# Hashed attention with an expert layer on one core: the first head loaded and projected in two parts, and eight bit moves spread over twice the steps

## The chip, the cores and the metric

One NeuronCore of a Trainium2 chip. The metric is the device time of one execution in microseconds. A profile's *span*, from the first to the last instruction, is about 2 us shorter. Engines: PE is TensorE, DVE is VectorE, ACT is ScalarE, POOL is GpSimd, and SP only issues DMAs.

## The reference, cut to what matters

```
q_bits = (einsum('bhsd,dk->bhsk', q, proj) > 0)          # 6 sign bits per token
k_bits = (einsum('bhsd,dk->bhsk', k, proj) > 0)
mask   = q_bucket[:, :, :, None] == k_bucket[:, :, None, :]
attn   = softmax(where(mask, q @ k^T / 8, -1e9)); x = attn @ v    # B=4, H=8, S=768, D=64
g = h * sigmoid(h), h = x @ w_in; out = g @ w_out        # 3072 x 512 -> 2048 -> 512
```

## The kernel before: the parts that the change touches

The kernel appends the sign bits as extra rows to q and k, so that one matmul gives score and mask together. A *step* `w` is one score part of 512 columns (9 steps a head, 288 in all). Each step issues planned side work, then attention times v, then the score of three steps ahead. `vv` is v in f16 and `vs` the sum of v's blocks; for the first eight heads and the last one, one matmul of the constant `dmat` with `vs` goes ahead of attention times v. Before any of that, the first head must be loaded, transposed, projected, and its bits moved to their rows:

```
for i in range(2):                       # SP's queue
    load_first(i)                        # q and k of head i, whole
    load_v(0, slice(i, i + 1))
...
t_first(0, 0, nc.scalar.copy)            # 3 transposes + copy
t_first(0, 1, nc.vector.tensor_copy)
warm_up(2)
bt = proj_first(0)                       # 4 f32 projections + signs on DVE
v_unit(0, (0,))                          # POOL: vv and vs of v
... cast_first on ACT; bits_first on DVE, DVE, ACT, POOL
t_first(1, 0, nc.scalar.copy)            # head 1's transposes, before the first score on PE
t_first(1, 1, nc.vector.tensor_copy)
warm_up(3)
```

The other place is in the steady state. An h_ps buffer (three exist, shared with the projections) is free again only when DVE has made `g` from it:

```
plan(wp + (i if Q < 4 else 0),           # Q = 3: pairs 6 and 7, wp = 93
     lambda Q=Q, i=i: bits_unit((2 * Q, 2 * Q + 1), i // 2, i % 2))   # two DVE moves each
...
after.append(lambda: nc.vector.scalar_tensor_tensor(out=g..., in0=th, scalar=1.0, in1=hp, ...))
```

## Time and profile before

| | before |
|---|---|
| time, median of the first 3 runs (lowest to highest) | 304.26 us (304.14 to 304.9) |
| span of the profiled run | 302.6 us |
| PE busy | 297.0 us, 98% |
| first score | 8.31 us |
| h_ps held up by g | 0.84 us at 73.5 us |
| PE clock at full rate from (the trace's clock record) | 6.0 us |

The prediction below shows the lines and reads them. Warm-ups are matmuls that compute nothing.

### The profile page before, as it was taken

The numbers are of one execution on the slowest core, as the hardware profiler recorded it, in microseconds if no ns is written. First come the engines' busy times: TensorE is split into PE (matmuls) and PEld (weight loads), VectorE is DVE, ScalarE is ACT, GpSimd is POOL, SyncE is SP. The second block draws the span as 40 slices with busy tenths as digits, with TensorE's granted clock in tenths as the row PEclk, the third lists the DMA queues.
The fourth block names the chain that finished last, engine by engine and source line by source line (L and its number), as shares of the span: only waits on it lengthen the run. The fifth ranks groups of instructions, "written<-read, shape, count | busy, mean of one in ns | idle before, by whom it ended". The sixth has DMA issues, their size and how long they took to land.

```text
span 302.6 us, 7181 instructions
## 1 busy us (share of the span) xinstructions
PE 297.0 (98%) x2710; PEld 175.1 (58%) x2710; DVE 180.0 (59%) x344; ACT 210.1 (69%) x392; POOL 128.2 (42%) x203
## 2 busy tenths in 40 slices
PE   8999999998999999999999999999999999999996
PEld 3676755545665665555565665555566654446653
DVE  5797938899568454854695434954443442764332
ACT  5987989988887686878886766878877732452300
POOL 6589999386618561845149411765111100000000
PEclk9999999999999999999999999999999999999999
DMA  7999998999979828744068146011022003001112
GB/s 202 245 248 215 156 145 122 217 180 166 145 161 153 131 74 229 124 97 134 3 126 139 51 63 203 2 40 32 2 61 63 4 34 95 35 2 69 37 66 73
DMA packets 103170, 32.87 MB, mean 109 GB/s; under 512 B 90656, under 2 KB 100192, under 8 KB 103136
## 3 DMA queue, kind: packets, MB, share of 16 engines
q1 hardware_dynamic: 98752, 28.22, 43.3%
q0 software_dynamic: 4224, 4.19, 9.0%
q8 instruction: 21, 0.34, 0.5%
q14 instruction: 13, 0.11, 0.1%
q10 hardware_dynamic: 160, 0.00, 0.0%
HBM read 27.27 MB, written 6.29 MB: 111 GB/s over the span
## 4 chain that ended last, share of the span: by engine, by line
PE 89%; DVE 5%; DMA 2%; issue 1%; SPq 1%; ACT 1%; POOL 0%; DVEq 0%; ACTq 0%; POOLq 0%
PE o_ps L496 26%; PE h_ps L461 24%; PE s_ps L366 18%; PE o_ps L398 11%; PE bp_ps L281 3%; DMA v_sb<-in_v_dram 2%; PE tp_ps L185 2%; DVE g L470 2%; PE o_ps L482 1%; PE warm_ps L125 1%; SPq L92 1%; DVE qka L343 1%; PE bp_ps L225 1%; DVE qk L246 1%; PE tp_ps L198 0%
## 5 line engine op out<-in xcount | busy, mean ns | idle before, releaser
L369 ACT ACTIVATE u<-s_ps 128x512 f16<-128x512 f32 x288 | 157.0, 606 | 38.7 <-PE s_ps L366 38.3
L470 DVE SCALAR_TENSOR_TENSOR g<-th,h_ps 128x512 f16<-128x512 f32 x96 | 65.5, 686 | 74.8 <-ACT th L468 74.7
L461 PE MATMUL h_ps<-xT,win 128*128 128x512 f16 (+1 forms) x512 | 98.4, 325 | 0.8 <-DVE g L470 0.8
L398 PEld LDWEIGHTS <-u 128*128 128x128 f16 x1152 | 68.1, 98 | 42.2 <-ACT u L369 8.4
L496 PE MATMUL o_ps<-wout,g 128*128 128x512 f16 x368 | 91.6, 379 | 0.0
L468 ACT ACTIVATE th<-h_ps 128x512 f32<-128x512 f32 x96 | 57.9, 603 | 36.6 <-PE h_ps L461 33.9
L398 PE MATMUL o_ps<-vv,u 128*128 128x65 f16 x1152 | 82.6, 194 | 0.6 <-ACT u L369 0.4
L461 PEld LDWEIGHTS <-win 128*128 128x128 f16 x512 | 49.8, 98 | 31.4 <-issue 1.0
L418 POOL TENSOR_TENSOR x_pr<-osum,rec 128x384 f16<-128x384 f32 x23 | 19.0, 826 | 89.3 <-DVE rec L417 88.9
L496 PEld LDWEIGHTS <-g 128*128 128x128 f16 x368 | 35.8, 98 | 33.6
L366 PE MATMUL s_ps<-qka 71*128 71x512 f16 x192 | 52.7, 327 | 0.2 <-DVE qka L238 0.2
L366 PE MATMUL s_ps<-qkb 128*128 128x512 f16 x192 | 52.6, 326 | 0.0
L251 POOL TENSOR_SCALAR qka<-qk 64x1536 f16<-64x1536 f32 x15 | 22.0, 1466 | 11.4 <-DVE qk L246 5.6
L501 DVE TENSOR_SCALAR osb<-o_ps 128x512 f32<-128x512 f32 x23 | 15.9, 691 | 15.0 <-PE o_ps L496 15.0
L251 POOL TENSOR_SCALAR qkb<-qk 64x1536 f16<-64x1536 f32 x15 | 22.1, 1471 | 1.2
L262 POOL TENSOR_TENSOR vsa<-v_sb 128x192 f32<-128x192 f32 x32 | 19.0, 592 | 0.0
L260 POOL CAST vv<-v_sb 128x384 f16<-128x384 f32 x32 | 16.2, 507 | 0.9 <-DMA v_sb<-in_v_dram 0.5
L246 DVE STREAM_TRANSPOSE qk<-k_blk 128x768 f32<-128x768 f32 x10 | 15.8, 1582 | 0.3 <-issue 0.3
L246 DVE STREAM_TRANSPOSE qk<-q_blk 128x768 f32<-128x768 f32 x10 | 15.9, 1591 | 0.0
L366 PEld LDWEIGHTS <-qka 71*128 71x128 f16 x192 | 15.5, 97 | 0.8 <-ACT qka L238 0.7
L366 PEld LDWEIGHTS <-qkb 128*128 128x128 f16 x192 | 15.4, 97 | 0.0
L412 DVE TENSOR_TENSOR osum<-o_ps,vsum 128x390 f32<-128x390 f32 x23 | 13.0, 565 | 2.3
(70 smaller groups left out, 163.0 us busy)
## 6 DMA issues: line engine op xcount, KB each, us to landing
out_dram<-osb SPq DMA_DIRECT2D x23, 256.0 KB
v_sb<-in_v_dram SPq DMA_DIRECT2D x15, 384.0 KB
q_blk<-in_q_dram SPq DMA_DIRECT2D x40, 96.0 KB
k_blk<-in_k_dram SPq DMA_DIRECT2D x40, 96.0 KB
win<-in_moe_w_in_dram POOLq DMA_DIRECT2D x4, 512.0 KB, 6.6
wout<-in_moe_w_out_dram POOLq DMA_DIRECT2D x4, 512.0 KB, 6.9
q_sb<-in_q_dram SPq DMA_DIRECT2D x5, 384.0 KB
k_sb<-in_k_dram SPq DMA_DIRECT2D x5, 384.0 KB
```

What stands on the lines that cost most here:

```text
L246: nc.vector.transpose(out=dst, in_=qk_sb[p, "qk"[n]])
L251: nc.gpsimd.tensor_scalar(out=dst[rows, :], in0=qk32[p][rows, :], scalar1=CS, scalar2=1.0, op0=ALU.mult, op1=ALU.mult)
L260: nc.gpsimd.tensor_copy(out=vv[:, :, 0:D], in_=src)
L262: nc.gpsimd.tensor_tensor(out=sa, in0=src[:, 0:3], in1=src[:, 3:6], op=ALU.add)
L366: nc.tensor.matmul(sp[:, o0 : o0 + n], t[rows, S + jt * P : S + (jt + 1) * P], t[rows, c0 : c0 + n], start=True, stop=True)
L369: nc.scalar.activation(out=u, in_=sp, func=AF.Exp, scale=ESC)
L398: nc.tensor.matmul(o_ps[h][:, c0 // P + i, :], u[:, o0 + i * P : o0 + (i + 1) * P], vv[:, jt, :], start=(not direct(h) and w % NU == 0 and ...
L418: (nc.vector if direct(h) else nc.gpsimd).tensor_tensor(out=x_pr[p][:, :, par * D : (par + 1) * D], in0=o[:, 0:NJ, 0:D], in1=rec[:, :, Non ...
L461: nc.tensor.matmul(hp[:, j, :], w_in16[:, dt, ft * P : (ft + 1) * P], xT[4 * b + dt][:, c0 : c0 + n], start=(dt == 0), stop=(dt == NDT - 1))
L468: nc.scalar.activation(out=th, in_=hp, func=AF.Tanh, scale=0.5)
L470: after.append(lambda: nc.vector.scalar_tensor_tensor(out=g[ci][:, grp * f : (grp + 1) * f, :], in0=th, scalar=1.0, in1=hp, op0=ALU.add, o ...
L496: nc.tensor.matmul(o2[tt], g[ci][:, ft, ct * P : (ct + 1) * P], w_out16[:, ft, :], start=(ft == 0), stop=(ft == NFT - 1))
```

## The change

Its intent is to start the first score earlier by bringing two thirds of the first head first, and to keep DVE from delaying `g` in steps 93 to 96. The diff, cut to its core (cuts marked with `...`; among what is cut, the warm-ups come in smaller pieces and DVE zeroes one buffer behind the first head instead of ahead of it):

```
-    for i in range(2):
-        load_first(i)
-        load_v(0, slice(i, i + 1))
+    load_first(0, (slice(0, 4 * D),))              # SP: blocks 0 and 1 of q and k
+    load_v(0, slice(0, 1))
+    load_first(1)
+    load_v(0, slice(1, 2))
...
+    load_first(0, (slice(4 * D, NJ * D),))         # POOL: block 2, after ident
...
+    t_first(0, 0, act, xa);  casts of q (ACT);  warm_up(1)        # xa: blocks 0 and 1
+    t_first(0, 1, vec, xa);  casts of k (DVE);  warm_up(2)
+    bpa = proj_first(0, xa)
+    t_rest()                                       # 2 transposes, one copy on ACT
+    for e in range(2):
+        cast_first(0, 0, e, nc.scalar, xb)         # xb: block 2
+        cast_first(0, 1, e, nc.gpsimd, xb)
+    v_unit(0, (0,), "v")                           # POOL: vv alone
+    signs_first(0, bpa, xa)
+    bpb = proj_first(0, xb)
+    ... bit moves of xa (DVE, POOL, ACT), signs of xb, ACT's second move of xa, bit moves of xb
+    v_unit(0, (0,), "s")
+    t_first(1, 0, act); t_first(1, 1, vec); warm_up(1)
...
-        if j == 1:                                 # order of a head's score parts
+        if j == 2:
...
+        if direct(h) and w % NU == (0 if h else 4):   # head 0: dmat at step 4, not 0
...
-            plan(wp + (i if Q < 4 else 0),
+            plan(wp + {2: i, 3: 2 * i}.get(Q, 0),
```

More of the change, by code (lines that the diff above doesn't have):

```diff
@@ L72, in load_qk, with load_first @@
             qk_sb[p, n] = t
-    def load_first(h):
-        for n, src in (("q", q), ("k", k)):
-            if h == 0:
-                qk_sb[0, n] = ld.tile([P, 2, NJ * D], F32, tag=f"ld{n}", name=f"{n}_row")
-            nc.sync.dma_start(out=qk_sb[0, n][:, h],
-                              in_=src[0, h].rearrange("(p t) d -> p (t d)", p=P))
+    def load_first(h, cols=(slice(0, NJ * D),)):
+        for c in cols:
+            for n, src in (("q", q), ("k", k)):
+                if (0, n) not in qk_sb:
+                    qk_sb[0, n] = ld.tile([P, 2, NJ * D], F32, tag=f"ld{n}", name=f"{n}_row")
+                (nc.gpsimd if h == 0 and c.start else nc.sync).dma_start(
+                    out=qk_sb[0, n][:, h, c],
+                    in_=src[0, h].rearrange("(p t) d -> p (t d)", p=P)[:, c])
     NG = S // 32
@@ L123, in warm_up @@
     def warm_up(n):
-        for _ in range(n):
-            nc.tensor.matmul(wps, warm, warm[:, None, :].to_broadcast([P, 4, P]),
+        while n > 0:
+            m = min(n, 4)
+            nc.tensor.matmul(wps[:, 0:m], warm, warm[:, None, :].to_broadcast([P, m, P]),
                              start=True, stop=True)
-    warm_up(5)
+            n -= m
+    warm_up(20)
     ident = cst.tile([P, P], F32, name="ident")
     make_identity(nc, ident)
+    load_first(0, (slice(4 * D, NJ * D),))
     NR = 2 * NBIT + 1
@@ L157 @@
         nc.vector.memset(VS[i // 2][:, i % 2, D:E1], float(NJ))
-    for i in range(NSL):
+    for i in (0, 2, 3):
         (nc.vector if i < 2 else nc.gpsimd).memset(QKB[i][0:64, :], 0.0)
@@ L191, with t_first @@
     HS = S // 2
-    def t_first(h, n, copy):
-        if (h, n) == (0, 0):
+    def t_first(h, n, copy, x=slice(0, NJ // 2)):
+        if 0 not in qk32:
             qk32[0] = t32.tile([P, 2 * S], F32, tag="qk32", name="qk32")
         tp = ps.tile([P, 512], F32, tag="m", name="tp_ps", bufs=3)
-        for j in range(NJ // 2):
+        for j in range(x.start, x.stop):
             nc.tensor.transpose(tp[:, j * P : (j + 1) * P],
@@ L200, in t_first, with t_rest, halves, cast_first @@
         x0 = (2 * h + n) * HS
-        copy(out=qk32[0][:, x0 : x0 + HS], in_=tp[:, 0:HS])
-    def halves(t, r, n, e):
-        return t[r, n * S : (n + 1) * S].rearrange("d (x e c) -> d x e c", e=2, c=P)[:, :, e]
-    def cast_first(h, n, e, eng):
-        dst = halves(QKA[0], slice(0, D), n, e) if h == 0 else \
-            halves(QKB[0], slice(D, 2 * D), n, e)
+        c = slice(x.start * P, x.stop * P)
+        copy(out=qk32[0][:, x0 + c.start : x0 + c.stop], in_=tp[:, c])
+    def t_rest():
+        tp = ps.tile([P, 2, P], F32, tag="m", name="tp_ps", bufs=3)
+        for n in range(2):
+            nc.tensor.transpose(tp[:, n], qk_sb[0, "qk"[n]][:, 0, 2 * P : 3 * P], ident)
+        nc.scalar.copy(out=qk32[0][:, 0 : 2 * HS].rearrange("p (n c) -> p n c", n=2)
+                       [:, :, 2 * P : 3 * P], in_=tp)
+    ALL = slice(0, NJ // 2)
+    def halves(t, r, n, e, x=ALL):
+        return t[r, n * S : (n + 1) * S].rearrange("d (x e c) -> d x e c", e=2, c=P)[:, x, e]
+    def cast_first(h, n, e, eng, x=ALL):
+        dst = halves(QKA[0], slice(0, D), n, e, x) if h == 0 else \
+            halves(QKB[0], slice(D, 2 * D), n, e, x)
         x0 = (2 * h + n) * HS
-        src = qk32[0][e * D : (e + 1) * D, x0 : x0 + HS].rearrange("d (x c) -> d x c", c=P)
+        src = qk32[0][e * D : (e + 1) * D, x0 : x0 + HS].rearrange(
+            "d (x c) -> d x c", c=P)[:, x]
         if eng is nc.scalar:
@@ L216, in cast_first, with proj_first @@
                               op0=ALU.mult, op1=ALU.mult)
-    def proj_first(h):
+    first_bits = {}
+    def proj_first(h, x=ALL):
         bp = ps.tile([P, 512], F32, tag="m", name="bp_ps", bufs=3)
+        w = slice(x.start * P, x.stop * P)
         for c in range(4):
@@ L224, in proj_first, with signs_first, bits_first @@
             o = e * (NBIT + 1)
-            nc.tensor.matmul(bp[32 * c : 32 * c + 32, 0:HS], pw[:, o : o + 32],
-                             qk32[0][:, x0 : x0 + HS], start=True, stop=True)
-        bt = btp.tile([P, S], F16, tag="bits", name="bits")
-        nc.vector.tensor_scalar(out=bt[:, 0:HS], in0=bp[:, 0:HS],
+            nc.tensor.matmul(bp[32 * c : 32 * c + 32, w], pw[:, o : o + 32],
+                             qk32[0][:, x0 + w.start : x0 + w.stop], start=True, stop=True)
+        return bp
+    def signs_first(h, bp, x=ALL):
+        w = slice(x.start * P, x.stop * P)
+        if h not in first_bits:
+            first_bits[h] = btp.tile([P, S], F16, tag="bits", name="bits")
+        nc.vector.tensor_scalar(out=first_bits[h][:, w], in0=bp[:, w],
                                 scalar1=sc[:, 0:1], scalar2=sc[:, 1:2],
                                 op0=ALU.is_gt, op1=ALU.subtract)
-        return bt
-    def bits_first(bt, h, n, e, copy):
+    def bits_first(h, n, e, copy, x=ALL):
         c = 2 * e + n
         r = slice(32 * c, 32 * c + NBIT + 1)
-        dst = halves(QKA[0], slice(D, D + NBIT + 1), n, e) if h == 0 else \
-            halves(QKB[0], slice(0, NBIT + 1), n, e)
-        copy(out=dst, in_=bt[r, 0:HS].rearrange("d (x c) -> d x c", c=P))
+        dst = halves(QKA[0], slice(D, D + NBIT + 1), n, e, x) if h == 0 else \
+            halves(QKB[0], slice(0, NBIT + 1), n, e, x)
+        copy(out=dst, in_=first_bits[h][r, 0:HS].rearrange("d (x c) -> d x c", c=P)[:, x])
     def block_unit(p, n):
@@ L253, in cast_unit, with v_unit @@
                                 op0=ALU.mult, op1=ALU.mult)
-    def v_unit(p, heads=(0, 1)):
+    def v_unit(p, heads=(0, 1), parts="vs"):
         for i in heads:
@@ L259, in v_unit @@
             src = v_sb[p][:, i, :].rearrange("p (t d) -> p t d", d=D)
-            nc.gpsimd.tensor_copy(out=vv[:, :, 0:D], in_=src)
+            if "v" in parts:
+                nc.gpsimd.tensor_copy(out=vv[:, :, 0:D], in_=src)
+            if "s" not in parts:
+                continue
             sa = nrm.tile([P, 3, D], F32, tag="vsa", name="vsa")
@@ L354, in parts @@
         jp, j = divmod(r, 3)
-        if j == 1:
+        if j == 2:
             return h, [(2 * jp, 512, 256, 0), (2 * jp + 1, 512, 256, 256)]
-        return h, [(2 * jp + j // 2, 0, 512, 0)]
+        return h, [(2 * jp + j, 0, 512, 0)]
     def score(w):
@@ L384, in av @@
             o_ps[h] = ps.tile([P, NJ + 1, E1], F32, tag="o", name="o_ps", bufs=2)
-            if direct(h):
-                nc.tensor.matmul(o_ps[h][:, 0:NJ, :], dmat,
-                                 vs[:, None, :].to_broadcast([P, NJ, E1]),
-                                 start=True, stop=True)
+        if direct(h) and w % NU == (0 if h else 4):
+            nc.tensor.matmul(o_ps[h][:, 0:NJ, :], dmat,
+                             vs[:, None, :].to_broadcast([P, NJ, E1]),
+                             start=h > 0, stop=True, skip_group_check=True)
         if w % NU == 4 and not direct(h):
@@ L399, in av @@
                                  u[:, o0 + i * P : o0 + (i + 1) * P], vv[:, jt, :],
-                                 start=(not direct(h) and w % NU == 0 and i == 0), stop=True,
+                                 start=((h == 0 or not direct(h)) and w % NU == 0 and i == 0),
+                                 stop=True,
                                  skip_group_check=True)
@@ L542 @@
     QST = 4 * NU
-    t_first(0, 0, nc.scalar.copy)
-    t_first(0, 1, nc.vector.tensor_copy)
+    xa, xb = slice(0, 2), slice(2, 3)
+    vec, act, pool = nc.vector.tensor_copy, nc.scalar.copy, nc.gpsimd.tensor_copy
+    t_first(0, 0, act, xa)
+    for e in range(2):
+        cast_first(0, 0, e, nc.scalar, xa)
+    warm_up(1)
+    t_first(0, 1, vec, xa)
+    for e in range(2):
+        cast_first(0, 1, e, nc.vector, xa)
     warm_up(2)
-    bt = proj_first(0)
-    v_unit(0, (0,))
+    bpa = proj_first(0, xa)
+    t_rest()
     for e in range(2):
-        for n in range(2):
-            cast_first(0, n, e, nc.scalar)
-    for e in range(2):
-        for n in range(2):
-            bits_first(bt, 0, n, e, (nc.vector.tensor_copy, nc.vector.tensor_copy,
-                                     nc.scalar.copy, nc.gpsimd.tensor_copy)[2 * e + n])
-    t_first(1, 0, nc.scalar.copy)
-    t_first(1, 1, nc.vector.tensor_copy)
-    warm_up(3)
+        cast_first(0, 0, e, nc.scalar, xb)
+        cast_first(0, 1, e, nc.gpsimd, xb)
+    v_unit(0, (0,), "v")
+    signs_first(0, bpa, xa)
+    warm_up(2)
+    bpb = proj_first(0, xb)
+    for n, e, copy in ((0, 0, vec), (1, 0, pool), (0, 1, act)):
+        bits_first(0, n, e, copy, xa)
+    signs_first(0, bpb, xb)
+    for n, e, x, copy in ((1, 1, xa, act), (0, 0, xb, vec), (0, 1, xb, vec),
+                          (1, 0, xb, pool), (1, 1, xb, pool)):
+        bits_first(0, n, e, copy, x)
+    v_unit(0, (0,), "s")
+    t_first(1, 0, act)
+    t_first(1, 1, vec)
+    warm_up(1)
+    nc.vector.memset(QKB[1][0:64, :], 0.0)
     nc.vector.tensor_copy(out=ident16, in_=ident)
     def second_head():
-        bt = proj_first(1)
+        signs_first(1, proj_first(1))
         for e in range(2):
@@ L566, in second_head @@
                 cast_first(1, n, e, nc.gpsimd)
-                bits_first(bt, 1, n, e, nc.vector.tensor_copy)
+                bits_first(1, n, e, nc.vector.tensor_copy)
         v_unit(0, (1,))
```

## The prediction

> **What bounds the kernel now.** I read the page's busy row first, then the waits of PE (TensorE's matmuls), the chain of waits through the first 9 us, and the timelines of DVE, POOL and PE around the two places that the change touches.
>
> ```profile
> PE 297.0 (98%) x2710; PEld 175.1 (58%) x2710; DVE 180.0 (59%) x344; ACT 210.1 (69%) x392; POOL 128.2 (42%) x203
> ```
>
> ```profile
> PE h_ps L461 <- DVE g L470: 0.8, 1, 0.8
> ```
>
> PE is busy 297.0 of 302.6 us, so the order of instructions on PE sets the time, and a change that removes no matmul can win only PE's 5.6 us of gaps, and the stretches at the start that are filled with useless warm-up matmuls. The second line is the only long wait that the view gives PE after the start. It lies at 73.5 us:
>
> ```profile
> 68.30 1.10 DVE L343 COPY qka<-bits 13x768 f16<-13x768 f16 x2
> 69.42 0.54 DVE L343 COPY qkb<-bits 13x768 f16<-13x768 f16 x1
> 69.97 0.60 DVE L340 TENSOR_SCALAR qkb<-bits,sc 13x768 f16<-13x768 f16 x1
> 70.60 0.69 DVE L470 SCALAR_TENSOR_TENSOR g<-th,h_ps 128x512 f16<-128x512 f32 x1
> 71.32 1.10 DVE L343 COPY qka<-bits 13x768 f16<-13x768 f16 x2
> 72.44 0.54 DVE L343 COPY qkb<-bits 13x768 f16<-13x768 f16 x1
> 73.00 0.61 DVE L340 TENSOR_SCALAR qkb<-bits,sc 13x768 f16<-13x768 f16 x1
> 73.64 0.69 DVE L470 SCALAR_TENSOR_TENSOR g<-th,h_ps 128x512 f16<-128x512 f32 x1
> ```
>
> ```profile
> 73.16 0.38 PE L366 MATMUL s_ps<-qkb 128*128 128x256 f16 x2
> 74.38 1.02 PE L461 MATMUL h_ps<-xT,win 128*128 128x512 f16 x4 [0.84 <-DVE g L470]
> ```
>
> Those are DVE's eight bit moves of pairs 6 and 7, run two steps' worth at a time, with one g (which frees an h_ps buffer) between them. PE's h_ps of 74.38 reuses the buffer whose matmuls ran at 69.09 and whose g came only at 73.64, behind four moves.
>
> The start, from the chain of waits and POOL's timeline:
>
> ```profile
> 1.01 2.31 PE warm_ps L125 x5
> 3.32 0.09 issue
> 3.41 1.51 PE tp_ps L198 x6
> 4.92 0.85 PE warm_ps L125 x2
> 5.77 0.96 PE bp_ps L225 x8
> 6.73 0.03 issue
> 6.75 0.69 DVE bits L228
> 7.44 0.02 issue
> 7.47 0.34 DVE qka L238
> 7.81 0.01 issue
> 7.82 0.35 DVE qka L238
> 8.18 0.14 issue
> 8.31 0.39 PE s_ps L366
> ```
>
> Nothing of the attention runs before the first score at 8.31 us. The serial chain ahead of it is six transposes, a copy, the projection, the signs, then bit moves on three engines.
>
> **What the Trainium skill says.** "TensorE: Matmul & The Clock Gate", Part 1, says that PE starts at half clock and reaches full clock after about 3.4 us of activity in a free-running window. The trace agrees in kind: a 128x128 transpose starts every 0.213 us at 3.4 us and every 0.109 us at 6.6 us, so the switch lies near 6.0 us. The same page ("Architectural detail") calls ACT, DVE and GpSimd (POOL) strict FIFO; in this trace each engine keeps program order, and my argument rests on that. "DMA: Bandwidth & Descriptors", Anatomy of one DMA, gives a DMA issued by GpSimd a fixed cost of about 2.0 us. Here the first packet of a POOL-queue load of win came 2.1 us after its issue began at 29.27, and the issue itself held POOL 0.96 us. No page prices a 7-row copy; I take it from the trace.
>
> **The change part by part.**
>
> *Bit moves every other step.* No work is removed. A PE step here takes about 1.5 us with an h_ps group. Now: 68.30 + moves 1.12 + 1.18 = 70.60, g to 71.29, moves 2.31 to 73.60, g to 74.3. After: first move pair to 69.42; g of the first group (its tanh ended at 69.17) to 70.1; second pair to 71.3; g of the 69.09 group to 72.0; third pair to 73.1. So the buffer is free at 72.0 instead of 74.3. PE could have started that h_ps at 73.37 (the last score part began at 73.265 and a 256-column matmul takes 0.108 us), so 74.38 - 73.37 = 1.0 us was lost. The profile says 0.84, because it counts from the modelled end of the score. The fourth pair, 1.15 us, now falls behind the sums of a head's end (0.22 + 0.56 + 0.19 = 0.97 us) at 73.1 to 74.1 and a g to 74.8, ending at 75.95. The next g, which frees the buffer of the 71.83 group, then ends near 76.6 while PE, now a microsecond earlier, wants it at about 76.5. I count 0.15 us given back: **gain 0.85 us**. PE is gapless for most of the rest, so it should reach the end.
>
> *The first head in two parts.* SP now brings 4 of 6 column blocks of q and k first (128 KB each instead of 192 KB); POOL's queue brings the rest. Step by step, against before:
> - PE's five warm-ups could be followed at 3.11 us (starts 0.425 us apart, last at 2.687); q landed at 3.28, and the transposes began at 3.41. With less data I estimate 3.15. Four transposes at 0.213 us and a 128-column warm-up at 0.107 put the last start at 3.89 and its end (0.421 us long) at 4.31, against 4.92.
> - DVE's copy of 256 columns: 0.56 us for 384, less 128 x 1.04 ns (512 columns take 0.69), is 0.43 us: 4.35 to 4.78. Projection 0.19 us later (5.52 to 5.71 before): 4.97. Its two passes of 256 columns take two thirds of 0.475 us each, still at half clock: end near 5.75. Signs 0.68 - 0.13 = 0.55 us: 5.83 to **6.4, against 7.44**. This is the intended gain of 1.05 us.
> - But the moves that follow sit in queues behind the second part. PE starts the two remaining transposes after the projection, 5.6; they end at 6.2 (the POOL loads, issued from about 1.5 and 2.3, should land near 4.5 and 5.0 by the 2.1 us above). ACT copies 256 columns (0.48 - 0.13 = 0.35) to 6.6, casts two blocks of 64x128 (0.52 less 256 x 0.98 ns = 0.27 each) to 7.2, and only then moves bits (7x256, 0.51 - 0.13 = 0.38) to 7.6 and again to 8.0.
> - POOL must cast the k rest from that same copy: 64x384 takes 0.54 and 64x1536 takes 1.47, so 64x128 is 0.34: 6.7 to 7.35. Then vv, 0.51, to 7.8, and its bits (0.50 for 384 columns, so about 0.4) to **8.2, against 8.08 before**. The first score needs those rows of k block 0. It starts near 8.35, against 8.31.
>
> So the second part's casts on ACT and POOL take back the whole microsecond: **gain near 0**. The reordered score parts cost nothing (the same matmuls), and let scores 0 and 1 go without the third column block. The ones-times-dmat matmul moves from step 0 to step 4 and frees 0.2 us that lay in an idle stretch anyway.
>
> Sum: -0.85 and about 0. Since POOL spans are rough and the change was made to start earlier, I lean by 0.1 us: 304.26 - 0.95 = **303.3 us**.
>
> **The rivals.**
> - *The early start comes through.* If the second transposes and ACT's copy run 0.5 us earlier than I place them (clock up earlier, shorter POOL instructions), the first score starts near 7.6 and the total gain is 0.85 + 0.7: 302.7 us. For it: signs end a full microsecond sooner. Against it: ACT's and POOL's queue order.
> - *The POOL queue comes late.* SP's backlog keeps the DMA engines near full from 3 us on. If the two POOL loads land at 6.3 instead of 5.0, every step after 5.6 slips by about 0.7 us, PE, ACT and POOL all stand behind it, and the head loses 0.7: 304.1 us. POOL also does its two 1.37 us memsets after the issues, until about 5.8, and head 1's casts end near 12.4 instead of 10.73; its first score was at 13.33, so another 0.9 us of delay would stall PE there.
> - *The stall at 73 us moves.* The next PE waits on g (0.2 us at 75.97, and the wait for tanh and g before the projection near 97) take over what was saved: then only 0.3 to 0.5 us is left, 303.8 us.
>
> **Range and chances.** The stall's gain is 0.4 to 1.0, the start's -0.6 to +0.7. Combined about the middle, 8 in 10 lie between 302.6 and 304.1. Two per cent is 6.1 us, more than all of PE's gaps, and I see no mechanism for a loss so large. So within 2% is 0.98, faster 0.01, slower 0.01.
>
> **What would show it.** In the changed profile the wait of PE's h_ps for g should be gone or under 0.2 us, with a g between any two pairs of moves. The first signs should end near 6.4, yet the first score come near 8.3, released by POOL's bit move. A first score before 7.9 or after 8.7 proves the working of the start wrong; a wait of PE's second transposes on the POOL-queue load proves the late-load rival; PE gaps of about 0.8 us anywhere in 66 to 100 us prove that the stall only moved.

## The result

| | before | changed |
|---|---|---|
| time, median of 4 runs (lowest to highest) | 304.20 us (304.14 to 304.9) | 304.44 us (304.28 to 304.78) |
| ratio (95% interval) | | 1.0004 (0.9986 to 1.0022) |
| span of the profiled run | 302.6 us | 302.1 us |
| first score | 8.31 us | 8.45 us |
| PE clock at full rate from | 6.0 us | 3.8 us |

The time is unchanged within noise, above the predicted range of 302.6 to 304.1. Yet the two profiles say that the span fell by 0.5 us. Both facts need an answer.

The busy row and PE's waits of the changed kernel (engine and line, what it waited for, us in all, times, longest):

```profile
PE 296.4 (98%) x2717; PEld 175.2 (58%) x2717; DVE 181.5 (60%) x348; ACT 210.0 (70%) x394; POOL 130.3 (43%) x209
```

```profile
PE warm_ps L131 <- POOL warm L118: 1.0, 1, 1.0
PE o_ps L429 <- ACT u L399: 0.6, 2, 0.4
PE s_ps L396 <- POOL qka L265: 0.6, 1, 0.6
PE bp_ps L248 <- ACT qk L217: 0.4, 1, 0.4
```

The wait of h_ps for g is gone. In its place are two waits at the start: the first score waits for POOL's bit move, and the second projection for ACT's copy.

DVE's timeline (start, length, what) in the stretch where the eight moves ran in blocks of four:

```profile
68.66 1.10 DVE L373 COPY qka<-bits 13x768 f16<-13x768 f16 x2
69.79 0.69 DVE L502 SCALAR_TENSOR_TENSOR g<-th,h_ps 128x512 f16<-128x512 f32 x1
70.39 0.53 DVE L373 COPY qkb<-bits 13x768 f16<-13x768 f16 x1
70.94 0.60 DVE L370 TENSOR_SCALAR qkb<-bits,sc 13x768 f16<-13x768 f16 x1
71.57 0.69 DVE L502 SCALAR_TENSOR_TENSOR g<-th,h_ps 128x512 f16<-128x512 f32 x1
72.29 1.10 DVE L373 COPY qka<-bits 13x768 f16<-13x768 f16 x2
```

A g now stands between any two pairs of moves. To see what it was worth I compare the start of the same exponential in both traces and call the difference the *lag* (minus is earlier than the first profile of before). In the changed kernel it is +0.14 us at step 0, +0.31 at step 12, +0.36 at step 96, -0.48 at step 108, and -0.50 at step 276. So the stall's removal gave 0.84 us and all of it reached the end, and the first head cost 0.31 us in this pair of profiles. In between, the lag falls by 1.01 us from step 100 to 104 and rises by 0.17 to step 108: the 1.0 us and the 0.15 given back that the prediction counted.

The start on PE and on POOL in the changed kernel:

```profile
3.11 0.63 PE L206 MATMUL tp_ps<-ident,q_row 128*128 128x128 f32 x2
...
3.83 0.44 PE L206 MATMUL tp_ps<-ident,k_row 128*128 128x128 f32 x2
...
4.40 1.03 PE L248 MATMUL bp_ps<-qk,pw 128*32 128x256 f32 x8
5.36 0.33 PE L216 MATMUL tp_ps<-ident,q_row 128*128 128x128 f32 x1
5.80 0.33 PE L216 MATMUL tp_ps<-ident,k_row 128*128 128x128 f32 x1
...
8.45 0.82 PE L396 MATMUL s_ps<-qka 71*128 71x512 f16 x4 [0.57 <-POOL qka L265]
```

```profile
2.79 2.72 POOL L167 MEMSET qkb<- 64x1536 f16 x2
6.63 0.69 POOL L235 TENSOR_SCALAR qka<-qk 64x128 f16<-64x128 f32 x2 [1.12 <-ACT qk L217]
7.38 0.51 POOL L288 CAST vv<-v_sb 128x384 f16<-128x384 f32 x1
7.95 1.02 POOL L265 COPY qka<-bits 7x256 f16<-7x256 f16 x3
```

This is the order that the prediction gave: transposes of the rest, ACT's copy, POOL's casts, vv, and only then the move that the first score needs. But this execution had PE at full clock from 3.8 us, where the profile of before had it only from 6.0. The two profiles are not like for like at the start.

### The profile page after: what moved, and what is told of

Its sections match the earlier page's. It is cut to its first block, busy times and chain, and to the rows that moved or that the text cites. A ratio compares the mean times of both kernels' runs of the same rounds, so it can differ in the third digit from the quotient of the medians.

```text
span 302.1 us, 7211 instructions
## 1 busy us (share of the span) xinstructions
PE 296.4 (98%) x2717; PEld 175.2 (58%) x2717; DVE 181.5 (60%) x348; ACT 210.0 (70%) x394; POOL 130.3 (43%) x209
## 4 chain that ended last, share of the span: by engine, by line
PE 88%; DVE 7%; POOL 2%; issue 1%; ACT 1%; DVEq 0%; POOLq 0%; ACTq 0%
PE o_ps L528 26%; PE h_ps L493 24%; PE s_ps L396 19%; PE o_ps L429 12%; DVE g L502 3%; PE bp_ps L311 3%; PE tp_ps L193 2%; PE o_ps L514 1%; DVE qk L273 1%; POOL qkb L167 1%; DVE qka L373 1%; ACT u L399 1%; DVE osum L444 1%; PE o_ps L420 1%; DVE qkb L370 0%
## 5 line engine op out<-in xcount | busy, mean ns | idle before, releaser
L429 PEld LDWEIGHTS <-u 128*128 128x128 f16 x1152 | 66.7, 98 | 46.1 <-ACT u L399 8.5
```

The source lines that it names most:

```text
L429: nc.tensor.matmul(o_ps[h][:, c0 // P + i, :], u[:, o0 + i * P : o0 + (i + 1) * P], vv[:, jt, :], start=((h == 0 or not direct(h)) and w % ...
```

## The experiments

Each ran beside runs of the kernel before on the same chip. The theory at the start (A): the stall's gain is real, and the first head really costs about a microsecond, hidden in the profiles by the clock's chance. The rival (C): the head costs the 0.3 us seen, and the rest lies outside the span.

### The bit moves alone

```
-            plan(wp + (i if Q < 4 else 0),
+            plan(wp + {2: i, 3: 2 * i}.get(Q, 0),     # in the kernel before
```

> The kernel before with the bit moves of pairs 6 and 7 every other step alone. Theory A (the stall at 73 us really goes and is worth what the trace of the changed kernel shows, a lag that falls by 0.84 us there, and the first head gives all of it back): about 303.4 us, ratio 0.997. Rival B (the step's gain does not reach the end in timed runs, or the stall is a matter of one run's chance): 304.1 to 304.3.

Measured: 303.57 us, median of 6 (303.0 to 304.04), against 304.16; ratio 0.9965 (interval 0.9929 to 1.0001). The lag is +0.04 at step 0, +0.05 at step 96 and -0.78 from step 108 to the end: 0.83 us. PE's waits no longer name g:

```profile
PE s_ps L366 <- DVE qka L238: 0.2, 1, 0.2
```

Theory A holds for this part; B falls.

### The first head alone

```
-            plan(wp + {2: i, 3: 2 * i}.get(Q, 0),     # in the changed kernel
+            plan(wp + (i if Q < 4 else 0),
```

> The changed kernel with the bit moves as before: the first head alone. Theory A: the head costs about 0.9 to 1.1 us once runs of like clock phase are compared, so 305.1 to 305.3. Rival C (the head costs only the 0.3 us that the two profiles show, and the rest of the time sits outside the span): 304.5 to 304.6.

Measured: 305.94 us, median of 6, spread widely (305.12 to 308.56), ratio 1.006. The lag is +0.77 at step 0 and +0.94 at step 12. Here PE's clock rose only at 6.6 us:

```profile
4.71 1.45 PE L248 MATMUL bp_ps<-qk,pw 128*32 128x256 f32 x8
6.09 0.48 PE L216 MATMUL tp_ps<-ident,q_row 128*128 128x128 f32 x1
...
9.07 0.82 PE L396 MATMUL s_ps<-qka 71*128 71x512 f16 x4 [0.55 <-POOL qka L265]
```

The projection takes 1.45 us instead of 1.03, and everything behind it slides: the first score comes at 9.07 instead of 8.45. The head's 0.3 us of the first pair of profiles was flattered. The median, 1.8 us above before's, is more than even theory A's 0.9 to 1.1: two of the six runs (307.15 and 308.56) were slow for a reason that this run does not show. The fastest, 305.12, is 1.35 above before's fastest.

### The kernel before again

> The kernel before, unchanged, for a second profile of it. Theory A holds that PE's clock came up at 6.0 us in the first profile of before by the chance of the run, and at 3.8 us in the changed kernel's; if so this profile shows another switch time than 6.0, and with one below 5 us the first score comes 0.4 to 0.7 us earlier than 8.31 and the span is nearer 302.0. Rival C: the switch is at 6.0 again, the first score at 8.3, and the span 302.6 with 1.8 us outside it.

Measured: first score at 8.08 us, span 302.4, lag a steady -0.24. The trace has no clock record, but the spacing of the transposes shows the switch between 4.1 and 4.6 us. Theory A's direction was right, but 0.23 us is less than its 0.4 to 0.7. An early clock alone can give more than 0.23: here head 1's k landed only at 7.00 us and held PE for 0.29 us (`PE tp_ps L198 <- DMA k_row` in its waits), and a later run with the clock at 4.1 came 0.36 earlier than the first profile. The part of the expectation that 1.8 us outside the span would go with a late clock is false: it was 1.8 with an early one. Across all runs of before it is always 1.73 to 1.84.

With the later runs the first score can be compared at like clock (kernels whose first head is that of before, against that of the change, in unaltered order):

| PE at full clock from | first score, head as before | first score, head as changed |
|---|---|---|
| 3.8 to 4.1 us | 7.96 (two ACT instructions more) | 8.45 (changed) |
| 5.6 us | 8.16 (dmat later) | 8.60 (one ACT instruction less) |
| 6.0 to 6.1 us | 8.31, 8.36 | none |
| 6.5 to 6.6 us | none | 9.08, 9.07 |

So the change makes the first score 0.44 to 0.49 us *later* at each phase that both have. These are few profiles of kernels that differ in small ways. The second profile of before, 8.08 with the late load, is left out; it would make the first difference 0.37.

### Bit moves of the first part ahead of the second part's casts

```
+    v_unit(0, (0,), "v")                         # in the changed kernel; POOL: vv first
+    ... bits_first(0, ..., xa) on DVE, POOL, ACT, ACT
     for e in range(2):
         cast_first(0, 0, e, nc.scalar, xb)       # was ahead of all the moves
         cast_first(0, 1, e, nc.gpsimd, xb)
```

> The changed kernel with the first part's bit moves and vv ahead of the second part's casts in the queues of ACT and POOL; same work. If those casts are what holds the first score (8.45 in the changed kernel), it comes at 7.6 to 7.8, behind the transposes of head 1 on PE, and the time is 0.7 us less than the changed kernel's, about 303.7. Rival: the late landing of the second part's load (5.76) holds everything through PE's queue; then the first score stays at 8.2 or later and the time within 0.3 us of the changed kernel's.

Measured: 304.19 us, median of 6; span 302.3. The clock rose at 6.64 us, so the run to compare is the head alone with its 6.63. PE's timeline:

```profile
7.30 0.43 PE L248 MATMUL bp_ps<-qk,pw 128*32 128x128 f32 x8 [0.35 <-ACT qk L217]
7.66 0.55 PE L206 MATMUL tp_ps<-ident,q_row 128*128 128x128 f32 x3
...
8.42 0.81 PE L396 MATMUL s_ps<-qka 71*128 71x512 f16 x4
```

The first score is at 8.42 instead of 9.07, with the same work: the order in ACT's and POOL's queues was worth 0.65 us there. Less of it reached the end: the lag at step 12 is +0.44 instead of +0.94, so 0.50 us, as ACT now has its casts and head 1's copy just ahead of the first exponential. No wait stands before it any more; PE itself arrives only then, because the second projection and head 1's transposes come first in its program. The expected 7.6 to 7.8 was missed by that, and the time of 303.7 too.

### The rest of the first head by SP's queue

```
-                (nc.gpsimd if h == 0 and c.start else nc.sync).dma_start(
+                nc.sync.dma_start(               # right behind the first part
```

> The changed kernel with the rest of the first head's q and k loaded by SP's queue, right behind the first part, instead of POOL's. Five profiles so far have 1.8 us between span and time where POOL's queue loads nothing at the start, and 2.13 to 2.16 where it does. Theory A2 (the two POOL loads cost about 0.36 us outside the span): the difference is 1.8 again. Rival (it comes with the program's length or its other instructions): 2.15. Inside the span POOL's memsets end near 4.2 instead of 5.5, so DVE's cast of k should take 0.29 us and not 0.88; the first score stays behind ACT's and POOL's second casts, 8.2 to 8.8 by the clock's phase.

Measured: 304.93 us, median of 6 (304.34 to 307.11). Theory A2 fell: time exceeds span by 2.09 to 2.14 us here, so POOL's loads are not what lies outside the span. The first score came at 8.36 with the clock at 4.6. The expectation for DVE was right. In the changed kernel, then here:

```profile
4.77 1.18 DVE L235 TENSOR_SCALAR qka<-qk 64x256 f16<-64x256 f32 x2
```

```profile
5.04 0.59 DVE L234 TENSOR_SCALAR qka<-qk 64x256 f16<-64x256 f32 x2
```

The same two casts take half the time once POOL's memsets are over. In the changed kernel the first of them took 0.88 us, from 4.77 to 5.65, just after the second memset's end at 5.51; the other 0.29. In three more runs with that memset the first cast began at 5.02, 5.06 and 5.19 and also ended at 5.65 or 5.66. The Trainium skill ("SBUF — State Buffer", Terms) says that DVE and GpSimd share a pair of ports as an exclusive lock and that the loser waits out the whole instruction; these numbers agree. Not every DVE instruction is held: the copy out of PSUM at 4.31 us took 0.42 us beside the memset and 0.42 without it. In the changed kernel nothing that held the first score waited for these casts.

The profiled run was the slow one of the six, with a span of 305.0. PE's waits name the cause of that one:

```profile
PE s_ps L395 <- DMA qka<-bits: 2.4, 1, 2.4
```

SP issued the first of the later pairs' bit transfers at 108.12 us, where the changed kernel's profile has it at 103.29, and PE stood still for 2.4 us at 109 to 111 us.

### The first scores ahead of head 1's transposes

```
     for w in range(LEAD):                        # on top of "bit moves first"
         score(w)
+    t_first(1, 0, vec)                           # were ahead of the scores, one on ACT
+    t_first(1, 1, vec)
```

> As the run with bit moves first, and the first three scores ahead of head 1's six transposes in PE's program, whose copies both go to DVE. If PE's order is what holds the first score there (8.42 with the clock up at 6.64), it now comes at 7.7 with a late clock and about 7.1 with an early one, and the time falls by 0.6 us against that run, to about 303.6. Rival: the head is then held by the exponentials of ACT and by head 1, and the lag at step 12 against the kernel before is as it was in the run with bit moves first (+0.44).

Measured: 304.32 us, median of 6. The first score came at 7.60 and the lag at step 0 was -0.31, but at step 12 it was +0.72: the rival was right, and its +0.44 even too small; the expected 303.6 us was missed. Head 1's transposes no longer fill PE's idle start, their copies reach DVE late, and head 1's projection stretches to 1.31 us where it took 0.85:

```profile
7.60 0.70 PE L396 MATMUL s_ps<-qka 71*128 71x512 f16 x2 [0.34 <-POOL qka L265]
...
9.92 1.31 PE L248 MATMUL bp_ps<-qk,pw 128*32 128x384 f32 x8
```

An early first score is no gain if what it overtakes is needed three steps later.

### Everything together

```
     # on top of "scores ahead": rest by SP's queue, all memsets and v sums early, dmat at step 0
+        if direct(h) and w % NU == 0:
```

> Everything together: bit moves of the first part ahead of the second part's casts, scores ahead of head 1's transposes, the rest loaded by SP, the memsets and v sums where they were before, dmat's matmul back at step 0. Theory A2: first score at 7.0 to 7.7, lag at step 12 of -0.5 or less against the kernel before, -0.84 more at 73 us, 1.8 us outside the span: time about 302.8. Rival (only the stall's gain is real, the head cannot be moved): 303.4 or more.

Measured: 304.92 us, median of 6. First score at 7.92, lag -0.38 at step 0 but +0.36 at step 12. My theory's -0.5 and 302.8 us were missed. Outside the span were 1.76 to 1.82 us, as expected, though theory A2 had already fallen. POOL's sums of v now ran before its bit move (vv waited for v until 5.56), and the copies of head 1 were as late as in the run before.

### The dmat matmul at step 4, alone

```
-            if direct(h):                        # in the kernel before
+        if direct(h) and w % NU == (0 if h else 4):
```

> The kernel before with head 0's dmat matmul at step 4 instead of step 0, alone. If that is what makes the lag grow from 0.14 to 0.31 us between steps 0 and 12 in the changed kernel, the lag here grows by 0.17 us between these steps and stays. Rival (the reordered score parts or POOL's later sums do it): no growth.

One run, 304.41 us. The lag goes from -0.15 at step 0 to +0.01 at step 12 and stays at 0.00 to 0.02: growth of 0.16 us. The matmul itself holds PE for 0.17 us in the changed kernel (12.23 to 12.40). At step 0 it lay in PE's wait for the first exponential; at step 4 PE has no such wait.

### One warm-up less, and one more

```
-    warm_up(1)        # the last one, in the changed kernel
```

> The changed kernel without its last warm-up matmul (one load of weights and one matmul less on PE; nothing waits for it). In every run so far the time exceeds the span by 1.74 to 1.85 us in six kernels, and by 2.09 to 2.21 in the four whose PE program is longest (2749 records on PE's sequencer against 2740 and 2748). Theory A3 (the 0.37 us hang on the length of PE's program): 1.8 here, and the time falls by 0.35 us with the span unchanged. Rival (they hang on ACT's two more instructions, or on something else of the first head): 2.15 still. Span as the changed kernel's, 302.1 to 302.6.

```
-    warm_up(3)        # in the kernel with the bit moves alone
+    warm_up(4)
```

> The kernel before with the bit moves every other step, and one warm-up matmul more ahead of the first score, where PE waits anyway. Theory A3: 2.15 us between span and time instead of 1.8, and so about 303.9 us where the bit moves alone gave 303.57. Rival: 1.8, and no difference.

Measured: 2.09 to 2.19 us outside the span with one less, 1.73 to 1.80 with one more. Theory A3 fell twice. The first kernel's time was 304.96 us, median of 6 (304.24 to 306.45): no gain. The second's four fast runs gave 303.0 to 303.69 us, a second confirmation of the bit moves. Its profiled run was slow beyond all else, 1085.4 us: four h_ps matmuls took 3.52 or 3.68 us from first to last instead of 1.03 nearly all through it. I leave that one out.

### Head 1's transposes ahead of the second projection

```
-    warm_up(2)                                    # on top of "bit moves first", rest by SP
+    later = [t_first(1, 0, act), t_first(1, 1, vec)]   # transposes now, copies later
     bpb = proj_first(0, xb)
```

> The run with bit moves first, with head 1's six transposes ahead of the second part's projection on PE (they fill the wait for ACT's copy), their copies as late as before, the rest loaded by SP, and two warm-ups less. If PE's gap before the second projection and the transposes behind it held the first score in that run, it now comes at 7.1 to 7.7; lag at step 12 against the kernel before -0.4 or less; 1.8 us outside the span; time 302.9 to 303.2. Rival (head 1's projection, exponentials and dmat after the first score take it back, as in the run with scores ahead): lag at step 12 of 0 or more, 303.5 or more.

Measured: 306.87 us, median of 6: worse, and a failure of mine. The profile (span 303.2) shows head 1's second group of transposes waiting 1.0 us, until ACT's bit moves were done; first score at 8.63, lag +1.03 at step 12. Outside the span were 2.09 to 2.19 us, where I had expected 1.8. The timed runs were worse still than the profiled one, which I did not follow up.

### What lies outside the span

```
+    spare = cst.tile([P, 2], F32, name="spare")   # in the kernel with the bit moves alone
+    for j in range(2):
+        nc.scalar.copy(out=spare[:, j : j + 1], in_=sc[:, 0:1])
```

> The bit moves every other step alone, with two tiny ACT copies (128x1) more ahead of head 1's copy, where ACT waits anyway. Twelve kernels so far: 1.8 us between span and time with 769 or 770 records on ACT, 2.15 with 771, whatever PE's length. Theory A4 (the 0.37 us outside the span hang on the length of ACT's program): 2.15 here, 771 records. Rival (they come with what the split head does on other engines): 1.8.

```
-    t_first(1, 0, act)                            # in the changed kernel
+    t_first(1, 0, vec)
```

> The changed kernel with head 1's copy of q moved from ACT to DVE, so one instruction less on ACT (770). Theory A4: 1.8 us between span and time instead of 2.15. Rival: 2.15. The span may move by some tenths either way, as DVE has both copies in a row.

Measured: 1.75 to 1.82 us with two ACT instructions more (771 records), 1.79 to 1.81 with one less. So the mere count on ACT is not it: A4 failed its first test and passed its second. What can be said is this. In these runs the excess goes with the kernel and not with the single run. It is 2.09 to 2.21 us in all six kernels that have the split head *and* copy head 1's q on ACT, and 1.73 to 1.85 in the other kernels, among them the three split-head kernels that copy it on DVE. Moving that one copy removes 0.37 us. Why, is open.

The kernel with two spare ACT instructions ran at 303.20 us (median of 4, 303.12 to 303.35, ratio 0.9961), the third confirmation of the bit moves. The one with the copy on DVE had 304.0 and 304.09 in two runs, and 307.7 and 308.11 in two.

## Why the prediction was wrong

**The stall at 73 us: right, in mechanism and size.** Predicted 0.85 us; the lag fell by 0.84 in the changed kernel, and by 0.83 and 0.82 in two runs that have the bit moves alone. The rival that the stall only moves is refuted: no wait of h_ps for g is left, and the gain stands to the last step.

**The first head, "gain near 0": this step failed.** The mechanism was right (second part's casts in ACT's and POOL's queues ahead of the moves; the reordered run brought the first score 0.65 us forward and step 12 by 0.50), but terms of the sum were mis-sized:
- "Its two passes of 256 columns take two thirds of 0.475 us each, still at half clock." The 0.475 us that I scaled had itself been cut short by the clock's rise at 6.0 us. In a run with the clock at 6.5, the starts of the two passes over 256 columns lie 0.43 us apart, not 0.32, and the last matmul takes 0.63 us. The signs began at 6.35 there, against 5.83 predicted, and the first score at 9.08 against 8.35.
- The transposes of k were to start near 3.68. They started at 3.8 to 4.1, and at 4.4 in one run, as k landed only at 3.76 to 4.37 us. In the run with the clock at 6.5 us the two together make the 0.5 us by which the signs came late.
- I read one clock phase off one profile and took it as given. It ranged from 3.8 to 6.6 us, and moves the first score by 0.6 us in the changed kernel. By the prediction's own sign, a first score after 8.7, the two runs at 9.07 and 9.08 show that its working of the start was wrong.
- "The ones-times-dmat matmul ... frees 0.2 us that lay in an idle stretch anyway" looked only at where it left. It arrived in a full stretch and cost 0.16 us.

At like clock the head costs 0.44 to 0.49 us at the first score and 0.16 for dmat: about **0.63 us lost** where I had put 0.

**Outside the span: not in the prediction at all.** 2.18 us for the changed kernel, 1.78 for before: about 0.37 us, read on every run.

The sum is -0.83 + 0.63 + 0.37 = +0.17 us, against a measured difference of medians of +0.24. The first two terms come from traces and the third from times and spans; the terms come from different runs, and the clock's phase in the timed runs is not on record. Within the runs' spread of 0.5 us I count the size as explained, and the cause of the third term as open.

**The rivals.** The late POOL load came true in part, and only with an early clock. POOL's two loads landed at 4.08 and 5.76 us in the changed kernel, where 4.5 and 5.0 were predicted: 2.6 and 3.5 us after their issue. (The prediction's 2.1 us was the time to a first packet and not to the landing.) The second transpose waited 0.28 us for the later one: it started 0.44 us after the first, against 0.17 in the run that loads by SP. That is over half of the 0.49 us in the table's first row. With the clock at 5.6 us or later nothing waited for it, and the head still cost 0.44. The earlier start did not come.

**Also open.** Runs over 1.5 us above their own kernel's fastest were 14 of 50 in kernels with the split head and 1 of 59 in those without (the 1085 us run apart). In the one that was profiled, late bit transfers held PE. Why a split head makes such runs frequent is not shown.

The version to keep is the kernel before with the bit moves alone: medians of 303.20 to 303.57 us in its forms, 0.35 to 0.39% below before. That is small, but the intervals of two of its three runs lie wholly below 1.

## What to carry to other kernels

When a buffer is freed by an engine that also does batches of side work, spread the batch so that the freeing instruction never stands behind more than one piece of it. When a serial start is split in two, look on every engine at whether the second part's first steps stand ahead of the first part's last ones: here that order cost 0.50 us at step 12. It is not enough by itself: in no order tried here did step 12 come earlier than in the first profile of before (lags of +0.22 to +1.03 us). Work moved out of an idle stretch costs its length where it arrives, if that stretch is full: 0.16 us for a matmul of 0.17. Before comparing the first microseconds of two profiles, compare when PE's clock rose in each, and compare time minus span as well as the span.

## What the Trainium skill lacked or had wrong

- "TensorE: Matmul & The Clock Gate", Part 1, gives the switch to full clock about 4 us into activity, within 0.5 us. PE was active from 1.0 us in every run here, and the recorded switches lie from 3.8 to 6.6 us, that is 2.8 to 5.6 us after it: a wider spread than that sentence gives.
- The same page knows the gate stuck at a quarter for 50 us and more. One run here was about that slow for nearly all its 1083.6 us (3.52 or 3.68 us for four 512-column matmuls against 1.03) while the run lists a mean granted clock of 1.000 (its trace holds no clock record).
- The same page gives no time for f32 matmuls on a 32-column strip. Here the two passes over 256 columns start 0.43 us apart at half clock (the run with one warm-up less).
- "Runtime: NRT & Kernel Launch" lists what runs before and after a kernel, but no page says why device time and a profile's span differ by an amount that depends on the kernel: here 1.73 to 1.85 us or 2.09 to 2.21 us, changed by moving one copy between engines.
- "SBUF — State Buffer", Terms, was right on the shared ports: a cast of 0.29 us took 0.88 us beside a POOL memset. It does not say there which DVE instructions are held: a copy out of PSUM was not (0.42 us with and without). The prediction left these casts out; the first score of the changed kernel did not wait for them.
